# Filter mixing and maxout network on one core: unread products ahead of three kinds of wait, one table made a turn later, and the product stage of batch 1 three steps later

## The chip, the cores and the metric

The kernel runs on one core of one Trainium2 chip. The metric is device time in microseconds (us) of one execution. The engines are called TensorE (PE in the profile, PEld for its weight loads), VectorE (DVE), ScalarE (ACT), GpSimd (POOL) and the sync engine (SP), which issues transfers.

## The reference

```python
X = np.fft.rfft(x, axis=1)                 # x: 8 x 3072 x 256
Y = X * (filt_r + 1j * filt_i)[None]       # filters: 1537 x 256
y = np.fft.irfft(Y, n=3072, axis=1)
t = y.reshape(8 * 3072, 256)
g = np.maximum(t @ w1, t @ w2)             # 256 -> 1024
out = g @ w_out                            # 1024 -> 256
```

Each of 256 channels of each of 8 batches is convolved with its filter by a Fourier transform of length 3072, and the 24,576 rows then go through a maxout layer and an output layer.

## The kernel before

The Fourier transform of length 3072 = 128 x 24 is done as matrix products. Per batch there is a stage of 12 products with the table `C1` (`f1`, L358), a write to DRAM and a read back in another order (`ad`, then `bt`, `f1_read`, L370), a **product stage** (`gen_f2`, L381) in eight parts, and, after another turn through DRAM (`zd`, then `zr`, `z_read`, L376), the last transform (`s4`, L534). One part of the product stage issues eight products with the table `U` into two `px` tiles (L430), two VectorE products with the spread filter `F` (L435, `pq<-px,F`), and, one part later, 16 products with `VP` and `VQ` into two `pz` tiles (L411), which ScalarE copies (L415).

The maxout is relu(t(w1-w2)) + t w2: `moe_h` (L550) makes one eighth of the hidden layer of 512 rows and `moe_o` (L566) one eighth of the output of the tile of 512 rows before it. The **step** is the unit of the hand-made order: step 8*tt + j is part j of tile tt, with 48 tiles in all. A table `todo` says which pieces of the Fourier work of later batches are issued behind which step. `plan_f2(n, steps, z1, z0)` names the nine steps of a product stage and the two of its reads of `zr`; `in_f2` tells in which steps the relu of parts 1 and 5 goes to ScalarE and not to VectorE.

Before step 0 there is a **set-up**, in which batch 0 is transformed without a turn through DRAM while the tables are made. Its order is also written by hand. The pieces that matter here:

- `expand_f(g, ri, E)` (L120) spreads eight rows of the real (ri 0) or imaginary (ri 1) filter `Fs` over partitions with products with a selection matrix, and engine E copies them to `F`. With ScalarE it uses a two-bank tile of the tag "pa", with VectorE two one-bank tiles of the tag "px".
- `first_s1(c, E)` (L450) waits for block c of x, makes eight products into a two-bank tile `pa`, and E copies them to `At`.
- `first_t1(g, E)` (L459) transposes `At` into `bt`; `first_s2` (L476) makes the products with `U` and the filter products; `first_s3` (L495) those with `VP` and `VQ`.
- `tables_pe` (L308) transposes `U` (16 transposes into `pv`) and VectorE copies `VP`; `tables_q(h, E)` (L318) makes half h of `VQ` from `VP` with two products `pw` and a copy by E.
- `spin(pd, n)` (L329) issues n products of the zero matrix `Sp` of 128 x 512 that nobody reads. Before the change, 25 of them open the kernel, and one stands ahead of each `first_s3`.

There are two two-bank places in PSUM under the tag "pa" and four one-bank ones under "px" in the set-up; later there are six one-bank places shared by `ph`, `pa`, `px`, `pz` and `py`. The pool chooses the place of a tile when the program is built. [...]

Of the kernel before, what the change touches and what calls it, by code (L numbers as in the profile page):

```python
# [29 lines left out]
def kernel(  # L30
# [26 lines left out]
    V, S, G, TE = nc.vector, nc.scalar, nc.gpsimd, nc.tensor  # L57
# [30 lines left out]
    def bank2(shape, dtype, name, tag=None):  # L88
        if tag is None:
            ring.append(ring.pop(0))  # L90
            tag = ring[-1]
        return p2.tile(shape, dtype, tag=tag, name=name)
# [5 lines left out]
    def load_x(b, c):  # L98
        t_ = xpool.tile([128, 4, D], BF16, tag="xb", name="xb")
        src = x[b].rearrange("(p n) d -> p n d", n=N2)  # L100
        G.dma_start(out=t_, in_=src[:, 4 * c:4 * c + 4, :])  # L101
        xb[b, c] = t_
# [14 lines left out]
        G.dma_start(out=Fs[ri][:, 0:2], in_=src[:, 0:2])  # L117
        G.dma_start(out=Fs[ri][:, 15:16], in_=src[:, 15:16])

    def expand_f(g, ri, E):  # L120
        if E is V:
            pf = [p2.tile([128, 2, D], FP32, tag="px", name="pf", bufs=4) for _ in range(2)]
        else:
            p_ = bank2([128, 2, 2, D], FP32, "pf")
            pf = [p_[:, b] for b in range(2)]
        fs = Fs[ri]
        for b in range(2):
            for c in range(2):
                m = 4 * b + c
                TE.matmul(pf[b][64 * c:64 * c + 32], Sel[:, m], fs[:, 2 * g:2 * g + 2], start=True, stop=True)  # L130
                p0 = 64 * c + 32
                if g:
                    TE.matmul(pf[b][p0:p0 + 32], Sel[:, 7 - m], fs[:, 16 - 2 * g:14 - 2 * g:-1], start=True, stop=True)  # L133
                else:
                    TE.matmul(pf[b][p0:p0 + 32, 0], Sel[:, 7 - m + c], fs[:, 0], start=True, stop=True)
                    TE.matmul(pf[b][p0:p0 + 32, 1], Sel[:, 7 - m], fs[:, 15], start=True, stop=True)
        f_ = F[:, ri, :, 2 * g:2 * g + 2].rearrange("p b u d -> p b (u d)")
        if E is V:
            for b in range(2):
                V.tensor_copy(f_[:, b], pf[b].rearrange("p u d -> p (u d)"))  # L140
        else:
            evac(E, f_, p_.rearrange("p b u d -> p b (u d)"))
# [141 lines left out]
    def table_e(t1):  # L284
        V.tensor_scalar(t1, pid, 12.0, None, OP.is_equal)
        V.tensor_scalar(e0[:, 0:1], pid, 0.0, t1, OP.is_equal, OP.add)
        V.tensor_scalar(e0[:, 1:2], e0[:, 0:1], -1.0, 1.0, OP.mult, OP.add)
        V.tensor_scalar(e0[:, 0:1], e0[:, 0:1], -0.5, 1.0, OP.mult, OP.add)
        V.memset(F0[:, :, :, 0:1], 0.0)
# [13 lines left out]
    def fix_f():  # L303
        for ri in range(2):
            G.tensor_scalar(F[0:64, ri, 0, 0], F0[:, ri, 0], e0[0:64, ri:ri + 1], None, OP.mult)
        G.tensor_copy(F[0:64, :, 1, 0], F0[:, :, 1])

    def tables_pe():  # L308
        pv = bank2([128, 16, 2, 64], BF16, "pv")
        for u in range(16):  # L310
            TE.transpose(pv[:, u], U[:, 2 * u:2 * u + 2].rearrange("p c x -> p (c x)"), I128)
        V.tensor_copy(VP[:, :, :, 0:48], pv[:, :, :, 0:48])

    def table_g():
        pg = p2.tile([128, 128], BF16, tag="px", name="pg", bufs=4)
        TE.transpose(pg, C1, I128)
        S.activation(G1, pg, AF.Copy)

    def tables_q(h, E):
        pw = bank2([128, 2, 512], FP32, "pw")  # L320
        for k in range(2):
            TE.matmul(pw[:, k], SW, VP[:, 8 * h + 4 * k:8 * h + 4 * k + 4], start=True, stop=True)
        evac(E, VQ[:, 8 * h:8 * h + 8].rearrange("p u b n -> p (u b n)"), pw.rearrange("p k n -> p (k n)"))
# [9 lines left out]
    def spin(pd, n):  # L333
        for _ in range(n):
            TE.matmul(pd, Sp, Sp.rearrange("p (o x) -> p o x", o=1).to_broadcast([128, 4, 128]), start=True, stop=True)

    def prep_wd(k, w1f, w2f):
        G.tensor_tensor(Wd[:, k], w1f[:, k], w2f[:, k], OP.subtract)
# [108 lines left out]
    def zeros(out_, n):  # L447
        S.activation(out_, zero.rearrange("p (a b) -> p a b", a=1).to_broadcast([128] + n), AF.Copy)

    def first_s1(c, E):  # L450
        pa = bank2([128, 2, 2, 2, 4, T], FP32, "pa")
        for dh in range(2):
            for n in range(4):
                TE.matmul(pa[:, dh, :, :, n], xb[0, c][:, n, 128 * dh:128 * dh + 128],
                          Ct.rearrange("p (b a t) -> p b a t", b=2, a=2), start=True, stop=True)
        evac(E, At[:, :, 0:48].rearrange("p h (a n) t -> p h a (n t)", a=2)[:, :, :, 128 * c:128 * c + 128],
             pa.rearrange("p h b a n t -> p (h b) a (n t)"))

    def first_t1(g, E):  # L459
        pt = p2.tile([128, 2, 2, D], BF16, tag="px", name="pt", bufs=4)  # L460
        t0 = 8 * (g // 2) + 2 * (g % 2)
        for c in range(2):
            for i in range(2):
                for dh in range(2):
                    TE.transpose(pt[:, c, i, 128 * dh:128 * dh + 128],
                                 At[:, 2 * dh:2 * dh + 2].rearrange("p b m t -> p t (b m)")[:, t0 + 4 * c + i], I128)
        o = bt[0][0:ROWS, 8 * (g // 2):8 * (g // 2) + 8].rearrange("p (c u) d -> p c u d", c=2)[:, :, 2 * (g % 2):2 * (g % 2) + 2]
        evac(E, o.rearrange("p c u d -> p c (u d)"), pt[0:ROWS].rearrange("p c u d -> p c (u d)"))

    def evac(E, out_, in_):  # L470
        if E is V:
            V.tensor_copy(out_, in_)
        else:
            S.activation(out_, in_, AF.Copy)  # L474

    def first_s2(g, pool):  # L476
        px = [p2.tile([128, 2, D], FP32, tag="px", name="px", bufs=4) for _ in range(2)]
        for i in range(2):
            for k, c in QUADS:
                t_ = 8 * (g // 2) + 4 * c + 2 * (g % 2) + i  # L480
                TE.matmul(px[k][64 * c:64 * c + 64, i], U[64 * k:64 * k + 48, 4 * g + 2 * i + c],  # L481
                          bt[0][64 * k:64 * k + 48, t_], start=True, stop=True)
        if pool:
            xs = apool.tile([128, 2, D], FP32, tag="at", name="xs")
            S.activation(xs[0:FROWS], px[1][0:FROWS], AF.Copy)
        pq = []
        for k in range(2):
            pq.append(pqpool.tile([128, 2, 2, D], BF16, tag="pq", name="pq"))
            E, src = (G, xs) if k and pool else (V, px[k])
            E.tensor_tensor(pq[k][0:FROWS],  # L490
                            src[0:FROWS].rearrange("p (o i) d -> p o i d", o=1).to_broadcast([FROWS, 2, 2, D]),
                            F[0:FROWS, :, k, 2 * g:2 * g + 2], OP.mult)
        return g, pq
# [129 lines left out]
    sines_u(2)  # L623
    first_s1(3, S)
    expand_f(0, 0, V)
    first_s1(4, V)
    first_s1(5, S)
    expand_f(6, 0, V)
    expand_f(1, 1, S)
    table_e(t1)  # L630
    load_f0()
    patch_f0()
# [4 lines left out]
    for n, g in enumerate(order):  # L637
        pend.append(first_s2(g, n in (0, 1, 2, 4, 6)))
        if n < 6:
            first_t1(order[n + 2], V)  # L640
        if n == 0:
            tables_pe()
            tables_q(0, S)
            expand_f(2, 1, S)
        if n < 6:
            expand_f((0, 3, 4, 5, 6, 7)[n], 1, S)
        if n < 2:
            load_x(1, 4 + n)
        if n == 2:
            fix_f()  # L650
        if n == 3:
            tables_q(1, S)
        if n in (4, 6):
            prep_wd(n // 2 - 2, *wf)
        if n in (4, 5):
            prep_w(n - 4, V)
        if n > 5:
            prep_w(n - 4, S)
        if n == 5:
            table_g()  # L660
        if n > 1:
            first_s3(*pend.pop(0))
# [17 lines left out]
    def plan(step, fn, *a):  # L680
        todo.setdefault(step, []).append((fn, a))
# [10 lines left out]
    def plan_f2(n, steps, z1, z0):  # L692
        g = []

        def go():
            if not g:
                g.append(gen_f2(n))
            next(g[0], None)

        for s_ in steps:  # L700
            plan(s_, go)
        plan(z1, z_read, n, 1)
        plan(z0, z_read, n, 0)

    def spaced(first, gap, count):
        return [first + int(gap * i) for i in range(count)]
# [3 lines left out]
    for c in range(2, 12):  # L710
        plan(int(0.6 * (c - 1)), f1, 1, c, (S, V)[c % 2])
    plan(6, f1_read, 1)
    plan_f2(1, spaced(14, 2.1, 9), 25, 33)
    plan_x(2, spaced(8, 4, 6))
    plan_f1(2, spaced(34, 1, 12), 46)
    plan_f2(2, spaced(60, 2.5, 9), 74, 81)
# [10 lines left out]
        plan_f2(n, spaced(197 + o, 3.4, 9), 216 + o, 226 + o)  # L727

    def in_f2(step):
        return 0 <= step < 6 or 14 <= step < 34 or 60 <= step < 82 or 104 <= step < 130  # L730

    for tt in range(6 * B + 1):
        b, i = divmod(tt, 6)
        for j in range(8):
            step = 8 * tt + j
# [38 lines left out]
```

## Time and profile before

| | |
|---|---|
| median of 13 runs | 536.76 us (535.94 to 542.76) |
| the profiled execution's own time | 536.2 us |
| its span, first to last instruction | 534.4 us |
| TensorE busy | 515.0 us (96%) |
| ScalarE, VectorE, GpSimd busy | 336.1, 321.9, 77.6 us |
| mean granted clock of TensorE | 0.991 |
| set-up ends, step 0 begins | about 51 us into the span |

In the rows that follow, a row of the timeline has the start in us, the length in us, engine, line, operation, tiles, shape and count; in brackets stands how long the engine was idle before it, and what ended that. A row of the table of stretches has, for each engine, busy time and number of instructions, then the granted clock of TensorE (1.00 is full speed), the busy share of the transfer engines and GB/s. Line numbers are those of the kernel before.

### The profile page before, as it was taken

The page shows a single profiled execution, that of the slowest core. Times are in us where ns is not written, and L with a number is a line of the kernel's source. Part 1 is how long each engine was busy: PE and PEld are TensorE (multiplying, and loading weights), DVE is VectorE, ACT ScalarE, POOL GpSimd, SP SyncE. Part 2 cuts the span into 40 slices and gives each one's busy share as a digit, 9 for nine tenths or more (in the row PEclk, how much of TensorE's full clock was granted, in tenths as well). Part 3 has the DMA queues.
Part 4 walks back from the last instruction along what each step waited for, and adds up shares of the span by engine and source line. Part 5 has one row for each costly group of instructions (what it writes and reads, how often), then busy time and mean ns, then how long its engine had stood idle before and what let it go on. Part 6 is the DMA issues. An engine that isn't in the chain of part 4 may idle for free.

```text
span 534.4 us, 12238 instructions
## 1 busy us (share of the span) xinstructions
PE 515.0 (96%) x5202; PEld 347.4 (65%) x5202; DVE 321.9 (60%) x436; ACT 336.1 (63%) x597; POOL 77.6 (15%) x130
## 2 busy tenths in 40 slices
PE   8798989999999999999999999999999999999995
PEld 3455656666666766676666666676666666677774
DVE  8876679335873476437783678538773688443432
ACT  7586747765787478855775467655776566545540
POOL 6575011021001100021001110021000000000000
PEclk9898999999999999999999999999999999999998
DMA  7992497879578975599458975699467936421122
GB/s 145 285 184 42 145 155 167 211 212 207 121 218 234 194 184 139 188 217 217 139 169 194 235 184 128 194 199 231 129 171 212 151 110 158 114 94 78 41 80 78
DMA packets 68459, 87.57 MB, mean 164 GB/s; under 512 B 4082, under 2 KB 48756, under 8 KB 67412
## 3 DMA queue, kind: packets, MB, share of 16 engines
q1 hardware_dynamic: 52196, 44.84, 37.3%
q0 software_dynamic: 16208, 41.95, 30.3%
q8 instruction: 40, 0.66, 0.5%
q14 instruction: 15, 0.12, 0.1%
HBM read 54.79 MB, written 47.19 MB: 191 GB/s over the span
## 4 chain that ended last, share of the span: by engine, by line
PE 76%; DVE 1%; issue 0%
PE po L581 28%; PE ph L556 28%; PE po L576 7%; PE pz L411 4%; PE px L430 3%; PE py L540 3%; PE pa L376 3%; DVE pq L435 1%; DVE ot L583 0%
## 5 line engine op out<-in xcount | busy, mean ns | idle before, releaser
L561 ACT ACTIVATE gt<-ph 128x512 bf16<-128x512 f32 x308 | 182.4, 599 | 111.5 <-PE ph L556 111.1
L581 PE MATMUL po<-Wo,gt 128*128 128x256 bf16 x1536 | 229.8, 273 | 0.0
L581 PEld LDWEIGHTS <-gt 128*128 128x128 bf16 x1536 | 150.3, 98 | 57.5
L435 DVE TENSOR_TENSOR pq<-px,F 120x1024 bf16<-120x1024 f32 x112 | 131.7, 1218 | 28.7 <-PE px L430 28.1
L583 DVE COPY ot<-po 128x512 f32<-128x512 f32 x96 | 66.2, 689 | 110.8 <-PE po L581 110.5
L556 PEld LDWEIGHTS <-Wd 128*128 128x128 bf16 x768 | 70.1, 98 | 27.8 <-issue 12.6
L588 POOL DMA_DIRECT2D out_dram<-ot x47 | 25.3, 538 | 432.9 <-DVE ot L583 406.5
L415 ACT ACTIVATE zt<-pz 112x512 bf16<-112x512 f32 x112 | 60.7, 594 | 42.0 <-PE pz L411 36.9
L559 DVE TENSOR_SCALAR gt<-ph 128x512 bf16<-128x512 f32 x76 | 52.1, 686 | 29.6 <-PE ph L556 22.5
L474 ACT ACTIVATE at<-pa 128x512 bf16<-128x512 f32 x78 | 46.8, 600 | 13.1 <-PE pa L376 11.6
L376 PE MATMUL pa<-xb,C 128*128 128x512 bf16 x84 | 31.8, 387 | 0.0
L540 PE MATMUL py<-G,zr 128*128 128x128 bf16 x384 | 29.8, 221 | 0.7 <-ACT zr L474 0.7
L411 PE MATMUL pz<-pq,VP 56*64 56x256 bf16 x448 | 28.4, 271 | 0.0
L411 PE MATMUL pz<-pq,VQ 56*64 56x256 bf16 x448 | 27.9, 268 | 0.0
L540 PEld LDWEIGHTS <-zr 128*128 128x128 bf16 x384 | 25.1, 99 | 3.7 <-issue 1.9
L101 POOL DMA_DIRECT2D xb<-in_x_dram x48 | 26.1, 551 | 1.8 <-DMA Fs<-in_filt_i_dram 1.7
L430 PE MATMUL px<-bt,U 48*64 48x256 bf16 x448 | 23.4, 281 | 2.1 <-DMA bt<-ad 2.0
L430 PEld LDWEIGHTS <-U 48*64 48x64 bf16 x448 | 8.2, 104 | 14.2 <-issue 11.6
L490 DVE TENSOR_TENSOR pq<-px,F 120x1024 bf16<-120x1024 f32 x11 | 13.2, 1221 | 5.6 <-PE px L481 3.5
L474 ACT ACTIVATE F<-pf 128x1024 bf16<-128x1024 f32 x10 | 10.1, 1023 | 6.7 <-PE pf L133 6.7
L411 PEld LDWEIGHTS <-VP 56*64 56x64 bf16 x448 | 13.2, 106 | 1.7 <-issue 1.7
L411 PEld LDWEIGHTS <-VQ 56*64 56x64 bf16 x448 | 13.2, 107 | 0.0
(381 smaller groups left out, 597.9 us busy)
## 6 DMA issues: line engine op xcount, KB each, us to landing
out_dram<-ot POOLq DMA_DIRECT2D x47, 512.0 KB, 4.1
xb<-in_x_dram POOLq DMA_DIRECT2D x48, 256.0 KB, 7.9
ad<-at SPq DMA_DIRECT2D x42, 256.0 KB
bt<-ad SPq DMA_DIRECT2D x28, 384.0 KB
zd<-zt SPq DMA_DIRECT2D x56, 192.0 KB
zr<-zd SPq DMA_DIRECT2D x14, 768.0 KB
wf<-in_moe_w_dram POOLq DMA_DIRECT2D x2, 1024.0 KB, 10.2
Fs<-in_filt_r_dram POOLq DMA_DIRECT2D x1, 768.0 KB, 6.8
```

The source lines that it names most:

```text
L376: TE.matmul(pa, C1, xb[b, c // 2][:, 2 * (c % 2):2 * (c % 2) + 2], start=True, stop=True)
L411: TE.matmul(pz[c][64 * k:64 * k + 64, i], W[64 * c:64 * c + 56, 2 * g + i, k], pq[k][64 * c:64 * c + 56, ri, i], start=(ri == 0), stop=(ri ...
L415: S.activation(zt[0:ROWS, c, o:o + 2], pz[c][0:ROWS], AF.Copy)
L430: TE.matmul(px[k][64 * c:64 * c + 64, i], U[64 * k:64 * k + 48, 4 * g + 2 * i + c], bt_[64 * k:64 * k + 48, t_], start=True, stop=True)
L435: V.tensor_tensor(pq[k][0:FROWS], px[k][0:FROWS].rearrange("p (o i) d -> p o i d", o=1).to_broadcast([FROWS, 2, 2, D]), F[0:FROWS, :, k, 2 ...
L474: S.activation(out_, in_, AF.Copy)
L540: TE.matmul(py[:, n], zr[b][:, 4 * i + n, 128 * dc:128 * dc + 128], G1, start=True, stop=True)
L556: TE.matmul(ph, Wd[:, dc, 128 * j:128 * j + 128], y_[:, dc].rearrange("p a b -> p (a b)"), start=(dc == 0), stop=(dc == 1))
L559: V.tensor_scalar(gt[tt][:, j], ph, 0.0, None, OP.max)
L561: S.activation(gt[tt][:, j], ph, AF.Relu)
L581: TE.matmul(p_, g_[:, jj, 128 * n:128 * n + 128], Wo[:, jj], start=False, stop=(jj == 7))
L583: V.tensor_copy(ot[tt][:, n - 1:n + 1], po[tt])
```

## The change

- `first_s1` puts one unread product into its tile `pa` before the products that wait for x, two for blocks 4 and 5.
- `expand_f(1, 1, S)`, the first spread of the imaginary filter, gets two of them ahead of its own products; with it the imaginary spreads of the first turn stand ahead of the products with the table `VP`.
- `tables_q(0, S)` moves from the first turn of the set-up's loop, where it stood ahead of `expand_f(2, 1, S)`, to the end of the second.
- The product stage of batch 1 moves from steps 14, 16, ... 30 to 17, 18, 20, ... 32, its reads of `zr` from steps 25 and 33 to 28 and 34, and `in_f2` accordingly.

```diff
-    def expand_f(g, ri, E):
+    def expand_f(g, ri, E, sp=0):
...
         fs = Fs[ri]
+        spin(pf[0].rearrange("p u d -> p (u d)"), sp)
...
-    def first_s1(c, E):
+    def first_s1(c, E, sp=1):
         pa = bank2([128, 2, 2, 2, 4, T], FP32, "pa")
+        spin(pa[:, 0].rearrange("p b a n t -> p (b a n t)"), sp)
...
-    first_s1(4, V)
-    first_s1(5, S)
+    first_s1(4, V, 2)
+    first_s1(5, S, 2)
     expand_f(6, 0, V)
-    expand_f(1, 1, S)
+    expand_f(1, 1, S, 2)
...
         if n == 0:
             tables_pe()
-            tables_q(0, S)
             expand_f(2, 1, S)
...
-        if n == 3:
-            tables_q(1, S)
+        if n in (1, 3):
+            tables_q(n // 2, S)
...
-    plan_f2(1, spaced(14, 2.1, 9), 25, 33)
+    plan_f2(1, spaced(17, 1.9, 9), 28, 34)
...
-        return 0 <= step < 6 or 14 <= step < 34 or 60 <= step < 82 or 104 <= step < 130
+        return 0 <= step < 6 or 17 <= step < 35 or 60 <= step < 82 or 104 <= step < 130
```

The whole difference in the built program is 10 products with their 10 weight loads more on TensorE, the moved instructions, and other places in PSUM for many tiles behind them.

## The prediction

> **What bounds the kernel now.** I read the page first, then TensorE's timeline, the stretches, and the timelines of ScalarE and VectorE in the two places that the change touches.
>
> ```profile
> PE 515.0 (96%) x5202; PEld 347.4 (65%) x5202; DVE 321.9 (60%) x436; ACT 336.1 (63%) x597; POOL 77.6 (15%) x130
> PEclk9898999999999999999999999999999999999998
> PE 76%; DVE 1%; issue 0%
> ```
>
> TensorE is the bound: 96% busy, and behind 110 us the waits charged to its products are 2.2 us in six places. What is gained before that is handed on whole to the end. The other two rows show where time can lie: the clock dips in the second and fourth slice, inside the set-up.
>
> ```profile
> 17.36 0.61 PE L454 MATMUL pa<-Ct,xb 128*128 128x128 bf16 x8 [1.43 <-ACT At L474]
> 19.08 0.55 PE L130 MATMUL pf<-Fs,Sel 96*32 96x512 bf16 x1 [0.57 <-ACT At L474]
> 20.04 1.93 PE L465 MATMUL pt<-I,At 128*128 128x128 bf16 x16
> 23.09 0.73 PE L465 MATMUL pt<-I,At 128*128 128x128 bf16 x8
> 26.11 0.59 PE L322 MATMUL pw<-VP,SW 128*128 128x512 bf16 x2 [1.39 <-DVE VP L312]
> 27.81 0.38 PE L130 MATMUL pf<-Fs,Sel 96*32 96x512 bf16 x1 [0.57 <-ACT VQ L474]
> 28.37 0.41 PE L481 MATMUL px<-bt,U 48*64 48x256 bf16 x8
> 26.74 1.02 ACT L474 ACTIVATE VQ<-pw 128x1024 bf16<-128x1024 f32 x1 [2.35 <-PE pw L322]
> ```
>
> These are the set-up's gaps: 1.43 + 0.57 + 1.39 + 0.57 us. In the third, TensorE has `pw` in front of the spreads and waits for `VP`, while ScalarE stands idle for 2.35 us.
>
> ```profile
> 15.79:19.20 3.41, 1.41 (x23) 0.86 (x24) 3.38 (x6) 2.55 (x5) 2.47 (x4) 0.99 1.13 210
> 19.20:22.61 3.41, 3.41 (x32) 1.82 (x25) 2.33 (x8) 1.02 (x1) 1.60 (x3) 0.51 1.06 385
> 22.61:26.02 3.41, 2.11 (x36) 1.60 (x32) 2.77 (x4) 1.51 (x2) 1.54 (x1) 1.00 1.06 328
> 46.52:49.93 3.41, 2.20 (x74) 1.75 (x74) 1.54 (x3) 2.36 (x4) 2.23 (x3) 0.99 0.30 25
> 49.93:53.34 3.41, 3.17 (x19) 2.08 (x19) 1.29 (x2) 1.80 (x4) 0.00 (x0) 0.51 0.75 136
> 66.99:70.41 3.42, 2.02 (x14) 1.18 (x12) 1.09 (x2) 0.78 (x2) 0.00 (x0) 1.00 1.23 168
> ```
>
> The two half-clock spells start 30.7 us apart, nine times 3.41 us, so I cut the time at those edges. A stretch with 1.41 us of TensorE work is followed by one at half clock; stretches with 2.02 and 2.11 us are not. (The one with 2.20 us is: mostly 48-column products and transposes.)
>
> ```profile
> 71.15 0.41 PE L430 MATMUL px<-bt,U 48*64 48x256 bf16 x7 [2.00 <-DMA bt<-ad]
> 73.55 0.41 PE L430 MATMUL px<-bt,U 48*64 48x256 bf16 x8
> 71.60 2.36 DVE L435 TENSOR_TENSOR pq<-px,F 120x1024 bf16<-120x1024 f32 x2 [3.52 <-PE px L430]
> ```
>
> The product stage of batch 1 starts (step 14) before `bt` is back: TensorE has finished step 14 at 68.55, starts at 68.86, and stands 2.00 us until 71.15.
>
> **The change, part by part.** I keep the clock of the trace before and move the events.
>
> *Unread products.* A product of 512 columns takes 0.21 us at full clock (25 in about 7.75 us, the first ones slower). Ten make 2.1 us if none were covered. For blocks 0 and 1, weight loads wait 0.70 and 0.62 us for x: covered. For blocks 2 and 3 some 0.1 to 0.2 us each shows on TensorE, but VectorE copies spreads without a gap from 11.12 to 17.18 and ScalarE is busy to 17.31, so it ends in their queues: 0. For block 4 likewise: TensorE is free from 15.93 to 17.36. For block 5 it is bare: the place of `pa` comes free at 17.31, so both products come after it and the block 0.43 us later; its `At` copy ends at 19.46, not 19.03. If ScalarE or VectorE were not full, the price would be up to 1.3 us more.
>
> For the first imaginary spread the built program tells something that the diff doesn't: before, `pf` sits where block 5's `pa` was and waits for ScalarE until 19.03; after, it sits where block 4's was, whose VectorE copy ends at 18.32. So its two products run at 18.8 to 19.2, behind the real spread, and it starts at about 19.2, as before.
>
> *The clock.* With this, the stretch 15.79 to 19.20 holds 15.79-16.35 and 17.36-19.20, 2.4 us of work, more than the two that kept the clock. Then spread, 16 transposes and the next spread run at full speed. From rows of that speed: spread 0.45, eight transposes 0.65, so 19.2 + 0.45 = 19.65, + 1.30 = 20.95, + 0.45 = 21.4, and the first products with `U` at 21.5 (VectorE's `bt` copy ends at 21.44) instead of 22.75: **-1.25 us**. Against this stand two rules of the Trainium skill, page "TensorE: Matmul & The Clock Gate". Its Part 1 has the clock halved only after a whole idle window of some 3.4 us. By it the 1.43 us gap costs no clock and filling gaps is worth nothing; the row shows the halving after 2.0 us of gaps in 3.41. Its Part 4 says that transposes don't count as work for the clock; then the coming stretch of 1.95 us of transposes would lose it again at 22.6. The stretch 22.61 to 26.02, nearly all transposes, kept 1.00. By the rules this part would be +0.1 us; I take the rows for the value and +0.1 for the bound.
>
> *`tables_q(0)` a turn later.* After: transposes of `U` 22.5-23.55, `VP` copied 23.8-24.75 (its VectorE queue is `pq`, `bt`, `VP`), spread 2 at 23.55 with no wait on `VP`, spread 0 at 24.8 (its place is that of `pv`), products with `U` of turn 2 at 25.2, not 28.37: -3.1. Then `pw` is inserted in turn 2 at about 26.65 (0.55 us), leaving -2.6 at turn 3. The reader that `VQ` now threatens is the first `first_s3`, in turn 3: ScalarE runs F(0) to 26.45, `xs` to 27.0, F(3) to 27.95, `VQ` to 28.9, so it starts at 28.95 (before 31.68). Next, F(5) is copied by 32.75 and the second `first_s3` starts at 32.8 against 35.23. From there TensorE has no gap over 0.2 us to 47.9, GpSimd's filter products and the weights (landed by 32 us) are early. **Set-up: -2.4 us**, of which -1.25 is clock, -1.15 this move. Bounds: +0.4 (all hidden but block 5) to -3.5.
>
> *Product stage from step 17.* Steps 15 to 17 take 0.98 us each in the rows, so `px` starts at 68.55 + 2.93 + 0.07 = 71.55 and `bt` landed by 71.1: the 0.31 + 2.00 us go; 0.4 us of margin. But the next part is now one step behind, at 18. Its `pz` need both VectorE products of the first part: 72.0 + 2.36 = 74.36. TensorE is there at 71.55 + 0.34 + 0.98 + 0.10 + 0.24 = 73.21: a **new wait of 1.2 us**, where before some 0.2 us is seen (73.79 to 74.0). ScalarE's relus, the copy of `ot` at 76.6 and step 20's part (VectorE free at 77.3, TensorE there at 77.0) stand behind it and fit. From step 20 the parts are at the old steps. Sum: -0.31 - 2.00 - 0.2 + 1.2 = **-1.3 us**; bounds 0 (`bt` late by 1.3 us more) and -2.5 (no wait). The reads of `zr` move in SP's queue behind two more writes of `zd`; the last one waits until some 5.9 us after the last `pz` (95.59 to 101.5 before), holds back the first `ad` write of the next batch by about 1.5 us, and all is needed ten steps later: 0. GpSimd's `out` and x loads come no later: 0.
>
> Sum: -2.4 - 1.3 = -3.7 us on 536.2, so 532.5 for such an execution. The median of the runs stands 0.56 us above that execution: 533.0.
>
> **Rivals.**
> 1. *The clock halves anyway*: the 2.20 us stretch at 46.52 speaks for it. Then -1.15 + 0.1 - 1.3 = -2.4: 534.4.
> 2. *`bt` still late, or the pile-up of two VectorE pairs lasts*, so that step 17 gives nothing: -2.4, 534.4. The 0.4 us margin speaks for it, the old positions from step 20 on against.
> 3. *The set-up's end is set elsewhere* (GpSimd, busy in 32-48 us) and nothing but step 17 counts: 535.5.
> 4. *Slower*: the pool has chosen other PSUM places for nearly all tiles behind the set-up. If in the product parts of the later batches `ph` or `pz` falls on a place that VectorE still reads, each of the 56 parts pays up to the 0.3 us that such waits cost now. At 0.066 us a part the gain is gone, at 0.3 it is 533.0 + 17 = 550; a tenth gives 539 to 540. Against it: in the trace these waits come to 2.3 us in seven places, all next to `s4`, whose position is unchanged.
>
> **How the numbers follow.** The forecast 0.56 (533.0; alone 531.5 to 534.0), rivals 1 and 2 together 0.24 (534.4), 3 0.12 (535.5), 4 0.08 (540). About 0.5%, 2.7 us, is what a measurement of this kernel tells from no change: faster is below 534.1. That is most of the forecast, and part of rivals 1 and 2: 0.63 faster; 0.29 same; 0.08 slower. The range 531.2 to 536.4 leaves out rival 4 and a tenth on the other side.
>
> **What would show it.** Right: clock 1.00 through 19 to 23 us, products with `U` of turn 2 near 25 us, no `pw` wait on `VP`, no `bt` wait at the product stage, and a wait of 1.2 us for `pq` at its second part. Wrong: a half-clock spell in 16 to 30 us, `first_s3` waiting for `VQ`, `px` waiting for `bt`, or TensorE waits behind 110 us above 3 us.

## The result

| | before | changed |
|---|---|---|
| median | 537.55 us (48 runs, 534.89 to 542.8) | 531.70 us (11 runs, 531.56 to 533.6) |
| ratio | 1 | 0.9892, 95% interval 0.9866 to 0.9917 |
| profiled execution: time, span, mean clock | 536.2, 534.4, 0.991 | 531.56, 529.8, 0.998 |

The change is worth 1.08%. The two profiled executions differ by 4.6 us, the medians by 5.85. The runs of before also spread over 8 us, those of the change over 2. (The median of before ahead of the prediction, 536.76 us, was that of 13 runs; 537.55 is that of 48.)

The page of the changed kernel, as before:

```profile
PE 513.5 (97%) x5212; PEld 346.7 (65%) x5212; DVE 321.6 (61%) x436; ACT 336.0 (63%) x597; POOL 77.7 (15%) x130
PEclk9999999999999999999999999999999999999999
```

The two dips of the clock are gone. TensorE's timeline in the set-up (start, length, instruction, idle before it; the last row is ScalarE's). Line numbers from here on are those of the kernel that ran; the changed kernel's stand one to three higher than those of before.

```profile
17.65 0.59 PE L336 MATMUL pa<-Sp 128*128 128x512 bf16 x2 [1.00 <-ACT At L476]
19.17 0.60 PE L336 MATMUL pf<-Sp 128*128 128x512 bf16 x2
20.25 1.24 PE L467 MATMUL pt<-I,At 128*128 128x128 bf16 x16
21.97 0.41 PE L483 MATMUL px<-bt,U 48*64 48x256 bf16 x8
25.23 0.38 PE L131 MATMUL pf<-Fs,Sel 96*32 96x512 bf16 x1 [0.77 <-DVE VP L313]
25.79 0.41 PE L483 MATMUL px<-bt,U 48*64 48x256 bf16 x8
33.00 0.38 PE L336 MATMUL pz<-Sp 128*128 128x512 bf16 x1 [0.59 <-ACT F L476]
28.38 1.02 ACT L476 ACTIVATE VQ<-pw 128x1024 bf16<-128x1024 f32 x1
```

The row of before for the first products with `U`:

```profile
22.75 0.41 PE L481 MATMUL px<-bt,U 48*64 48x256 bf16 x8
```

The 16 transposes take 1.24 us and not 1.93, and the first products with `U` start at 21.97, not 22.75; one wait of 0.77 us stands where 1.39 + 0.57 stood; the products with `U` of turn 2 start at 25.79, not 28.37, and the second `first_s3` at 33.00, not 35.23. The set-up's first `s4` starts 2.2 us earlier (47.95, before 50.17). The spell at half clock behind it is absent in this execution, and step 14 ends 3.3 us earlier (65.25, before 68.55).

In the product stage of batch 1:

```profile
68.28 0.42 PE L431 MATMUL px<-bt,U 48*64 48x256 bf16 x8
69.71 0.41 PE L431 MATMUL px<-bt,U 48*64 48x256 bf16 x8
70.02 0.29 PE L412 MATMUL pz<-pq,VP 56*64 56x256 bf16 x1
71.15 0.30 PE L412 MATMUL pz<-pq,VP 56*64 56x256 bf16 x3 [0.84 <-DVE pq L436]
68.74 4.61 DVE L436 TENSOR_TENSOR pq<-px,F 120x1024 bf16<-120x1024 f32 x4 [1.61 <-PE px L431]
```

No product waits for `bt`. The new wait is there, 0.84 us, behind two pairs of VectorE products that follow each other without a gap. The first product of the next stage (step 34) starts 4.8 us earlier (95.26, before 100.08), so the stage gave 1.5 us; the last products of the kernel start 4.65 us earlier (522.12, before 526.77), so less than 0.2 us was lost in the 427 us between, for all the other places in PSUM.

### The profile page after: what moved, and what is told of

It reads as the page before. It is cut to its first block, busy times and chain, and to the rows that moved or that the text cites. A ratio compares the mean times of both kernels' runs of the same rounds, so it can differ in the third digit from the quotient of the medians.

```text
span 529.8 us, 12255 instructions
## 1 busy us (share of the span) xinstructions
PE 513.5 (97%) x5212; PEld 346.7 (65%) x5212; DVE 321.6 (61%) x436; ACT 336.0 (63%) x597; POOL 77.7 (15%) x130
## 4 chain that ended last, share of the span: by engine, by line
PE 76%; DVE 1%; issue 0%
PE po L583 28%; PE ph L558 28%; PE po L578 7%; PE pz L412 4%; PE px L431 3%; PE py L542 3%; PE pa L377 3%; DVE pq L436 1%; DVE ot L585 0%
## 5 line engine op out<-in xcount | busy, mean ns | idle before, releaser
L542 PE MATMUL py<-G,zr 128*128 128x128 bf16 x384 | 29.4, 219 | 0.7 <-ACT zr L476 0.7
```

What stands on the lines that cost most here:

```text
L542: TE.matmul(py[:, n], zr[b][:, 4 * i + n, 128 * dc:128 * dc + 128], G1, start=True, stop=True)
```

## The experiments

The change has three parts: U, the ten unread products; T, the later table; S, the later product stage. Times are medians; each ratio is to runs of the kernel before that belong to it.

| kernel | us | ratio (95% interval) | mean clock of its runs |
|---|---|---|---|
| U | 538.59 | 1.0005 (0.997 to 1.004) | 0.981 to 0.994 |
| T | 535.63 | 0.9952 (0.9924 to 0.998) | 0.985 to 0.994 |
| S | 534.82 | 0.9949 (0.9917 to 0.9981) | 0.976 to 0.995 |
| U+T | 535.10 | 0.9944 (0.992 to 0.9967) | 0.991 to 0.998 |
| T+S | 532.16 | 0.9908 (0.988 to 0.9936) | 0.989 to 0.998 |
| U+T+S, the change | 531.70 | 0.9892 (0.9866 to 0.9917) | 0.993 to 0.999 |

The first four ran on one chip, with a kernel before of 537.88 us in the median of 35 runs; T+S ran on another, with 536.64 us in 11. The intervals of T and S alone reach from 1.0 us to 4 us and more, so the sizes below are medians and not sharp values.

**U alone.** The new arguments of `expand_f` and `first_s1` with their products, and nothing else of the diff.

> The kernel before with the ten unread products alone. Theory A (they keep the clock between 19 and 23 us, which the rows price at 1.25 us, and cost nothing else): 1.2 us less than the kernel before, granted clock 1.00 from 19 to 23 us, first products with U at about 21.5 to 22 us instead of 22.75. If the half-clock spell at 50 us goes with it, 1 us more, so down to -2.3. Theory B (the clock rule by whole idle windows, so that they fill nothing): +0.1 to +0.4 us, the spell still there or absent for another reason. Theory C (the clock is the whole gain of the set-up): -3.3 us.

538.59 us, no gain; the runs fall apart in 535.8 to 536.9 (five, clock 0.993 to 0.994) and 538.3 to 542.5 (seven, clock 0.981 to 0.988). In the profiled execution the spell at 19 us is gone and the first products with `U` start at 21.94 us, as theory A says. But cut at the edges of its spell, the table of stretches (columns as before: stretch, busy time of PE, PEld, DVE, ACT, POOL, then clock, transfer share, GB/s) reads

```profile
23.44:26.85 3.41, 1.59 (x19) 0.62 (x16) 1.72 (x3) 1.05 (x2) 2.67 (x2) 1.00 1.09 290
26.85:30.26 3.41, 3.25 (x36) 1.62 (x35) 1.52 (x2) 2.54 (x4) 0.56 (x1) 0.51 1.34 211
30.26:33.68 3.42, 3.42 (x33) 1.31 (x31) 2.13 (x3) 1.99 (x3) 3.40 (x3) 0.50 1.19 215
40.50:43.92 3.42, 3.42 (x53) 1.89 (x52) 2.15 (x3) 1.32 (x2) 2.97 (x2) 0.50 0.01 2
```

The wait of 1.41 us for `VP` now fell in a stretch with 1.59 us of work, and the half clock that followed lasted five stretches, 17 us, although TensorE was busy in all of them. So the gain of one place was lost at the next gap. None of the three theories had that.

**T alone.** `tables_q(0, S)` from turn 1 to turn 2.

> The kernel before with the first half of VQ made a turn later, alone. Theory A: -1.15 us in the set-up (second first_s3 at about 34.1 instead of 35.23), with the half-clock spell from about 19 to 22.6 us still there. Theory C: 0, since at half clock the transposes and not the table are late. Under either, the reader of VQ (the first first_s3) does not wait for it by more than 0.2 us.

535.63 us: 2.25 us less than before, twice what theory A had, though the interval (1.1 to 4.1 us) just takes its 1.15 us in; theory C's 0 falls. No product waits for `VQ`. In the profiled execution half clock ran from about 18 to 25 us and again from 69 to 76 us, the second behind the wait for `bt`. Its times too follow its clock, from 533.9 us at 0.994 to 538.1 at 0.985.

**S alone.** `spaced(17, 1.9, 9), 28, 34` and the bounds of `in_f2`.

> The kernel before with the product stage of batch 1 from step 17, alone. Theory A (the 2.3 us wait for bt goes, a wait of 0.8 to 1.2 us for the VectorE products of the first part comes): -1.3 to -1.5 us, both half-clock spells of the set-up as before. Rival: the stage moved at no gain and the set-up had given all: 0 (within 0.3).

534.82 us: 3.06 us less in the median, 2.7 by the ratio, again twice theory A, with an interval (1.0 to 4.5 us) that takes theory A in. Its profiled execution has a spell from 18 to 25 us and none behind it, not even that at 50 us.

**U and T, product stage from step 14.**

> The change without its third part: unread products and the later table, product stage as before from step 14. Theory A: the set-up gains are additive, -2.4 us and, where the spell at 50 us stays away, -3.3; the wait for bt at the product stage is there again at 2.0 us (the transfers move with the set-up). Rival: the transfers of x and of bt do not move with the set-up, so the wait at step 14 grows by what the set-up gains, to 4 to 5 us, and the run gains nothing over the kernel before.

535.10 us. The two waits for `bt` are 0.38 + 2.18 us, not 4 to 5, so the transfers moved with the set-up and the rival falls. The longer wait, and the stretches at the edges of its spell:

```profile
68.48 0.64 PE L431 MATMUL px<-bt,U 48*64 48x256 bf16 x7 [2.18 <-DMA bt<-ad]
64.90:68.32 3.42, 1.02 (x7) 0.49 (x5) 0.10 (x1) 0.60 (x1) 0.00 (x0) 1.00 1.23 165
68.32:71.73 3.41, 3.25 (x16) 1.53 (x17) 2.57 (x3) 0.60 (x1) 0.00 (x0) 0.50 1.13 143
```

The wait for `bt` is not only its 2 us: here one stretch holds nearly all of it, and the next 3.41 us run at half clock. Before's own profiled execution had the wait cut in two by an edge (2.02 and 2.67 us of work) and showed nothing of it.

**The wait for `bt` filled.** U and T, product stage from step 14, with

```diff
         px = [ps.tile(...) for _ in range(2)]
+        if b == 1 and g == 4:
+            for _ in range(9):
+                TE.matmul(px[0].rearrange("p u d -> p (u d)"), C1, U[:, 0:8].rearrange("p t x -> p (t x)"), start=True, stop=True)
```

> The set-up of the change with the product stage as before from step 14, and nine unread products of 128 x 512 in front of the first part's products, in the 2.2 us wait for bt. Theory A: the wait keeps its length, 2.2 to 2.6 us, but the half-clock spell behind it (68.3 to 71.7 us) is gone: 0.5 to 1.5 us less than without them, 533.6 to 534.6 us, clock 0.997 or above. Theory B (the spell comes from the transfers or from something else than idle time): 535.1 us, the spell stays.

533.64 us, ratio 0.9921 (0.9892 to 0.9949), against 0.9944 without them: 1.2 us less, though the products with `U` came no earlier (from the end of step 14 to the seven that waited, 3.3 us, without them 3.0). No spell lies behind them:

```profile
66.22:69.63 3.41, 2.48 (x21) 1.16 (x19) 0.90 (x1) 0.36 (x1) 0.00 (x0) 1.00 1.23 149
69.63:73.04 3.41, 3.41 (x42) 2.07 (x40) 3.41 (x5) 2.07 (x5) 0.77 (x2) 1.00 0.74 93
```

The edges here are carried back from the half clock at the end of the span. About 0.9 of the 2.48 us are the nine products (65.02 to 67.13 us); without them some 1.6 us would be left (an estimate from these rows), as little as in stretches that lost the clock. The intervals of the two kernels overlap, so the size is open; with the trace, theory A has the better of it.

**The wait for `VP` filled.** U, and six more unread products ahead of `pw`:

```diff
         pw = bank2([128, 2, 512], FP32, "pw")
+        spin(pw[:, 0], 6 if h == 0 else 0)
```

> The kernel before with the ten unread products and six more ahead of the products pw, in the 1.4 us wait for VP; the table stays in the first turn. Theory A (what the later table gives is above all a gap less at the edge of the clock's threshold): the 17 us half-clock spell of the ten alone, 26.9 to 43.9 us, is gone in nearly every run, and the median falls from 538.6 to about 534.5 us, with the 1.4 us wait for VP and the 0.57 us wait for VQ unchanged. Theory B (the order itself counts): the spell or its loss stays, 538 us or above.

535.96 us, ratio 0.9981 (0.9953 to 1.0008): between the theories. In the profiled execution no spell is left before the end of the span, so the 17 us are gone. Five of twelve runs are at 537.4 to 538.8 us with a clock of 0.988 to 0.991; the wait for `bt` is still in this kernel, but whether it is the cause is open, since these runs have no profile. At full clock, this kernel shows what the order alone is worth:

```profile
17.90 0.59 PE L337 MATMUL pa<-Sp 128*128 128x512 bf16 x2 [1.01 <-ACT At L477]
27.16 0.38 PE L131 MATMUL pf<-Fs,Sel 96*32 96x512 bf16 x1 [0.57 <-ACT VQ L477]
34.60 0.38 PE L337 MATMUL pz<-Sp 128*128 128x512 bf16 x1 [0.59 <-ACT F L477]
```

From block 5's unread products to the second `first_s3` it is 16.70 us here and 15.35 in the change: 1.35 us for the order of the table.

**Without the products ahead of blocks 0 to 3.** `first_s1(c, E, sp=0)`, the six others kept.

> The change without the four unread products ahead of blocks 0 to 3; the six ahead of blocks 4 and 5 and of the imaginary spread stay. Theory: the stretches before 15 us are full of products anyway and the four only lie in waits for x: the same as the change, 531.7 within 0.3 us, clock 1.00 through the set-up. Rival (they too hold the clock): a half-clock spell from somewhere in 12 to 16 us and 1 to 2 us more.

532.27 us, ratio 0.9887 (0.9852 to 0.9921) against 0.9892: the same. The four do nothing that these runs can tell. Its profiled execution has a spell, from 48 to 52 us, behind the two gaps at the end of the set-up, and not where the rival had it.

**The change without its unread products (T+S).**

> The change without its ten unread products: the later table and the later product stage alone. Theory: the half-clock spell behind the gap at 16 to 19 us is there in most runs and lasts one or two stretches of 3.41 us; the gaps behind it are as short as in the change. 533.5 to 534.5 us, 2 to 3 us above the change. Rival (the unread products are worth nothing where the two other parts are in): 531.7 us.

532.16 us, ratio 0.9908: 0.5 us more than the change in the medians, 0.9 by the ratios, and the two intervals overlap, so it isn't shown that the unread products are worth anything here. The spell behind the gap at 16 to 19 us is there, one stretch long. Cut at its edges:

```profile
16.41:19.82 3.41, 1.96 (x28) 1.13 (x29) 3.38 (x7) 2.00 (x3) 2.17 (x3) 1.00 1.09 228
19.82:23.23 3.41, 3.41 (x36) 2.01 (x35) 2.05 (x7) 1.70 (x2) 1.59 (x3) 0.50 1.04 405
```

But it costs less than I had it: from block 5's `pa` to the second `first_s3` it is 16.24 us here (17.29 to 33.53), 0.9 more than in the change. The theory misses; the median is near the rival's.

**The product stage at every second step from 16**, `spaced(16, 2, 9), 28, 34`.

> The change with the product stage of batch 1 at steps 16, 18, ... 32, every second step, instead of 17, 18, 20, ... 32. By the rows of the change, bt lands 0.4 to 0.6 us after step 16 is done and 0.4 us before step 17 is. Theory: a wait of about 0.5 us for bt at the first part comes, the 0.84 us wait for VectorE at the second part goes: 0.3 us less than the change, some 531.4 us. Rival: bt lands later when it is asked for earlier, a wait of 1 us or more and no gain, 532 us or above.

533.19 us, ratio 0.9901 (0.9865 to 0.9936): the rival. The wait for `bt` is 1.03 us and not 0.5, with no gain. The profiled execution had the spell at 48 to 52 us besides.

**The product stage at every second step from 17**, `spaced(17, 2, 9), 28, 35`.

> The change with the product stage of batch 1 at steps 17, 19, ... 33, every second step, and the second read of zr at step 35. Theory: bt has landed and the second part comes two steps behind the first, so neither the wait for bt nor the 0.84 us wait for VectorE is there: 0.8 us less than the change in the stage, some 531 us. Rival: at odd steps the copies of the output tile fall on the same steps as the parts, and VectorE's queue makes the products wait at each of four such steps for up to 0.69 us: 532 to 534 us.

529.96 us (529.62 to 531.2), ratio 0.9875 (0.9849 to 0.9900): the lowest median of all, and ahead of the change by 1.7 us in the medians and 0.9 by the ratios, with intervals that overlap. By the rows it is 1.3: the 0.84 us wait is gone, so are the two waits of `ph` for VectorE beside `s4` (0.7 us together in the change), since `s4` is at even steps; a wait of 0.24 us for `bt` came. Of the changed kernel's `pz` wait this is left:

```profile
68.54 0.41 PE L431 MATMUL px<-bt,U 48*64 48x256 bf16 x7 [0.24 <-DMA bt<-ad]
70.94 0.41 PE L431 MATMUL px<-bt,U 48*64 48x256 bf16 x8
71.18 0.51 PE L412 MATMUL pz<-pq,VP 56*64 56x256 bf16 x4
```

The rival's waits of up to 0.69 us behind the copies of the output tile are not there.

**Unread products in the two gaps at the end of the set-up.** The change with

```diff
+    spin(bank2([128, 2, 512], FP32, "pd")[:, 0], 4)
     first_t2h(V, 0)
...
+    pd = ps.tile([128, 512], FP32, tag="ps", name="pd")
+    for _ in range(4):
+        TE.matmul(pd, C1, U[:, 0:8].rearrange("p t x -> p (t x)"), start=True, stop=True)
     s4(0)
```

> The change with four unread products of 512 columns in each of the two gaps at the end of the set-up (0.77 us ahead of the last transposes, 0.69 us ahead of the first s4). Theory A (what spread is left in the runs of the change, 531.6 to 533.6 us, is the half-clock spell from about 48 to 52 us, which comes or not by where the stretches of 3.41 us fall): the slow half of the runs goes, all between 531.5 and 532.3 us plus up to 0.3 us for what sticks out of the gaps, clock 0.997 or above in each. Rival (the spread is the transfers'): as before, 531.6 to 533.6 us.

532.70 us (532.05 to 533.94), ratio 0.9925 (0.99 to 0.9951): 1.0 us above the change in the medians, with intervals that overlap. The clock is 0.996 to 0.998 in every run, about as theory A says. But the runs still spread over 1.9 us, so what spread is left in the change isn't shown to be the clock's, and nothing is won:

```profile
48.15 1.02 PE L678 MATMUL pd<-U,C 128*128 128x512 bf16 x4 [0.68 <-ACT zr L476]
49.01 0.61 PE L542 MATMUL py<-G,zr 128*128 128x128 bf16 x8
```

These are the second four; the first four did run inside their gap, which is gone. The place in PSUM of the second four, one of those that the set-up had held until then, came free only with the copy that `s4` itself waits for. So they ran behind the wait and not in it: 0.86 us on the path.

**Both together.**

> The two edits before together: unread products in the two gaps at the end of the set-up, and the product stage at 17, 19, ... 33. Theory: they add, since one is worth clock in the set-up and the other a wait behind it: 530.7 to 531.2 us in nearly every run. Rival: one of the two gains is the other's loss, 531.7 us or above.

530.75 us (530.50 to 531.14), ratio 0.9886 (0.9862 to 0.9910): within the theory's range, but 0.8 us more than the stage at 17, 19, ... alone on the same chip, so there are no two gains that add. The second four products stand behind the same wait as before, again for 0.86 us.

## Why the prediction was right, and where it was not

The direction, the order of size and the moved waits stand. The sum was 2.15 us too small (3.7 against 5.85). The predicted time was only 1.3 us off (533.0 against 531.70), because the median of before rose by 0.8 us with more runs. That 531.70 lies inside the range is in part luck: what lowered the median beyond the predicted sum, the clock in the runs that have no trace, stood nowhere in it.

*The direct steps.* From block 5's start to the second `first_s3`, it was 17.87 us (17.36 to 35.23) and is 15.35: 2.52 us less, predicted 2.4. Up to the first products with `U` that is 1.07 us for the unread products and the clock, predicted 1.25: the two products ahead of the imaginary spread ran at 19.17 to 19.70 us and not at 18.8 to 19.2, so the spread came later than said. The rest is 1.45 us for the table, predicted 1.15; at full clock on both sides (U with six more products) it measured 1.35. The changed execution reached block 5 some 0.3 us later, so 2.2 us arrive at the end of the set-up. `VQ` was done at 29.4 us and never waited for. The product stage: predicted -1.3, measured -1.5. Its new wait is 0.84 us and not 1.2, because one `pz` product ran before it, at 70.02 us, where the prediction had all of them wait for both VectorE products. ScalarE, the writes of `zd`, the reads of `zr` and the next stage took no harm that shows. Block 5 waited behind its two products as said, and block 4 cost nothing. Rivals 3 and 4 fell: TensorE's waits behind 105 us are 2.2 us in the change, as before. (Rival 4's tenth of a microsecond a part would make 538.6 us, not 539 to 540; nothing hangs on it.)

*The step that failed* is "I keep the clock of the trace before and move the events". It made the clock a property of one execution: one spell at 19 us that ten products remove, worth 1.25 us, and nothing anywhere else. Between the two traces this is nearly right but for the spell at 50 us, which was kept and is gone: some 1.1 us of their 4.6. Over the runs the term is mis-sized, and put on the wrong part of the change. The unread products are worth 0.5 us by the medians and 0.9 by the ratios (T+S against the change), which is not clear of noise, and alone they give no gain. T and S, for which I counted no clock at all, measured 2.25 and 2.7 to 3.06 us alone, about twice their rows. Each alone is not clear of its rows, but together they are: T+S is 3.4 to 6.4 us faster by its interval, against 1.35 + 1.5 by the rows. The spells lie behind stretches of 3.41 us with little work, and where the edges lie differs from run to run, so each gap of the kernel before had its chance: those at 16 to 19, 24 to 28, 48 and 69 us all have a spell behind them in one of these traces.

How much that makes: over 35 runs of before on one chip, the span follows the mean clock with a correlation of -0.96, at 0.385 us per thousandth (a straight line through their spans and clocks, 533.3 us at 0.994 to 540.9 at 0.975). Their median is 0.988, that of the change 0.998. Ten thousandths make 3.9 us; the 2.0 us that remain are near 1.35 + 1.5 less 0.43 for block 5's bare products. The parts fit the same line: the median clock of T's runs is 0.990 and of S's 0.992, so 0.8 and 1.5 us of clock with 1.35 and 1.5 us of rows make 2.1 and 3.0, measured 2.25 and 3.06; that of U's is 0.9875, no better than before. A mean clock also counts idle time at the end of the span, and the 11 runs of before on another chip give 0.52 us per thousandth, so I take this for a size and not for an exact division.

*The two rules weighed.* The rule of Part 1 of the page "TensorE: Matmul & The Clock Gate" of the Trainium skill, as the prediction took it (a whole idle window of about 3.4 us before the clock halves), does not hold here: the longest gap ahead of the spell in U alone was 1.41 us. Part 4 of that page (transposes don't count) does not fit before's stretch from 22.61 us either. Some 1.6 of its 2.11 us are transposes, not nearly all; had they not counted, 0.5 us of work would be left, less than in any stretch that kept the clock, and it kept it. Whether transposes help to end a spell is not settled.

Left open: in which share of the runs each gap costs its spell, since only one execution of each kernel has a trace; what besides busy time decides whether a stretch loses the clock; and whether U has a gain with S alone, which wasn't run.

## What to carry to other kernels

Price a TensorE gap with its clock, and over runs: where the times of one kernel spread by more than a per cent, set each run's time against its mean clock before reading a single trace. A gap that one profiled execution passes at full clock can be followed by 3.4 us or more of half speed in another: the gap at 48 us did so in two of the variants and not in the change. So here shortening several gaps was worth more than filling the worst one. Give unread products a place in PSUM that is free before the wait begins; and when a stage is moved past a late transfer, keep the distance between its first two parts.

## What the runs showed of the hardware

- The half clock comes in units of 3.41 us; the longest spell, in U alone, is 17.06 us. With each trace cut at the edges of its own spells, a stretch with 1.01 to 1.86 us of TensorE work was always followed by half clock (1.01, 1.41, 1.43, 1.56, 1.74, 1.86), the longest single gap being 2.18 us. From 1.87 to 2.25 us both happened: stretches with 1.87, 1.91, 1.92 and 1.94 us were passed, stretches with 1.95 (twice), 1.96 and 2.25 us were not. So the busy time alone does not decide it. Two of these, from S alone and from the run without the products ahead of blocks 0 to 3:

```profile
24.93:28.34 3.41, 1.91 (x23) 0.94 (x22) 1.54 (x2) 0.87 (x1) 2.40 (x2) 1.00 1.15 214
28.34:31.75 3.41, 3.20 (x52) 1.98 (x51) 1.82 (x2) 3.41 (x6) 0.85 (x1) 1.00 1.36 213
44.83:48.24 3.41, 1.95 (x48) 1.60 (x49) 0.98 (x2) 1.93 (x4) 1.61 (x3) 1.00 0.46 52
48.24:51.65 3.41, 3.41 (x18) 1.88 (x16) 1.80 (x3) 1.88 (x4) 0.00 (x0) 0.50 0.76 181
```

- Being busy does not end it at once: in U alone it went on for five stretches, though TensorE was busy for 3.25 to 3.42 us of 3.41 in each, mostly on transposes and products with part of the array.
- The mean clock of executions of the same kernel ranged from 0.975 to 0.994, and 0.385 us of span went with each thousandth.
- Unread products whose place in PSUM came free only with the copy that the next products wait for ran behind that wait, for 0.86 us.
